# Token weights issued behind the first batch's inputs, a new landing model and two priorities, in a linear attention and mixer kernel

## The chip, the cores and the metric

The kernel runs on one core of a Trainium2 chip. The metric is the device time of one execution in microseconds (us); the lower the better. A change within 2% counts as the same. Most executions of one kernel agree within a per cent. Some fall into a slower state (over 1.5% above the fastest of the same kernel, as a rule with a lower TensorE clock).

Engine names in the profile: PE is the TensorE matmul pipeline, PEld its weight loads, DVE is VectorE, ACT is ScalarE, POOL is GpSimd, SP is SyncE, which here only issues DMAs (SPq). "L230" is a line of the kernel file that was profiled, so the same statement has different numbers in different versions.

## The reference

A gated linear attention over 4 batches, 8 heads, 768 steps and head width 48, followed by a token and channel mixer. Cut to what matters:

```python
for t in range(S):                                   # the attention, per batch and head
    state = alpha[:, :, t, :, None] * state + einsum('bhd,bhe->bhde', k[:, :, t], v[:, :, t])
    y[:, :, t] = einsum('bhd,bhde->bhe', q[:, :, t], state)
# x: y with the heads side by side, (4, 768, 384)
h  = maximum(x.T @ w_tok1, 0) @ w_tok2               # over the tokens
u  = x + h.T
out = u + maximum(u @ w_ch1, 0) @ w_ch2              # over the channels
```

Inputs and output are float32: q, k, v and alpha are 4.7 MB each.

## The kernel before

Each batch is cut into 6 chunks of 128 tokens. A chunk needs four input tiles, `at` (alpha), `kt`, `qt`, `vt`, each 128 partitions by 8 heads by 48 float32. One tile is one DMA, and in it every piece that is contiguous in memory is one row of one head, 192 bytes. The tiles land in rings of 6:

```python
inp = pool("inp", NIN)                               # NIN = 6
def load(n, name, src, after=None):
    ...
        c[name] = inp.tile([128, H, D], F32, name=name)
        nc.sync.dma_start(c[name], src[b, :, ci * C : ci * C + C, :].transpose([1, 0, 2]))
    loads[n][name] = plan.op({"SP": 550}, emit, [after], takes=[name, "loads"], lands=196608 / RATE)
```

The kernel chooses the order of instructions itself. Every piece of work is registered with `plan.op`, with its engines, modelled duration, dependencies and priority; `Plan.issue` then runs a small list scheduler while the program is built, and emits the pieces in the order that it found. Its clock is a model. An engine runs its instructions in exactly that order, so if the model believes that a tile lands earlier than it does, an engine stands in front of that tile while other work waits behind it (in run h1 below PE does so for 4.17 us). The model of a landing:

```python
if o["lands"] and eng == "POOL":                     # a weight, issued by GpSimd
    first = max(heavy, start + 2900.0)
    heavy = first + o["lands"]
    o["end"] = heavy + 900.0
    ...
elif o["lands"]:                                     # an input tile or a store, issued by SP
    wire = max(wire, start + 1650.0) + o["lands"]
    o["end"] = wire + 900.0
```

The small constants and the weights:

```python
u128 = consts.tile([128, 128], BF16, name="u128")
make_upper_triangular(nc, u128, val=1.0, diag=True)
id128 = consts.tile([128, 128], BF16, name="id128")
...
RATE = 205.0                                         # GB/s of the input tiles, in the model
...
for n in range(NT):
    ...
    pkk, vb, acqm = chunk(n)
    if n == NCH - 2:
        weight("wt1", wt1, src1, acqm, 2.6)          # first token weight, during chunk 4 of batch 0
    if n == NCH - 1:
        weight("wt2", wt2, src2, pkk, 2.3)
        weight_ch1(0, vb); weight_ch1(1, vb); weight_ch1(2, vb)
    if n == NCH:
        weight_ch2(0, vb)                            # halves of the second channel weight
    if n == NCH + 1:
        weight_ch2(1, vb)
    if NCH - 1 <= n < NT - 1:                        # batch 1's inputs wait for wt2's landing
        load_ak(n + 1, hold_back(wload["wt2"], wload["wc12"]) if n == NCH - 1 else None)
        load_qv(n + 1)
```

Of the kernel before, what the change touches and what calls it, by code (L numbers as in the profile page):

```python
# [14 lines left out]
class Plan:  # L15
# [9 lines left out]

    def __init__(self, rings, cold, window, slack):
        self.rings = rings
        self.cold = cold
        self.window = window
        self.slack = slack  # L30
        self.ops = []
        self.taken = {r: [] for r in rings}
        self.asked = {r: [] for r in rings}
        self.mixed = ("pmix", "ptp", "pcum")

    def op(self, engines, emit, deps=(), prio=0, takes=None, frees=(), lands=0.0):
        o = {"eng": engines, "emit": emit, "deps": [d for d in deps if d is not None],
             "prio": (prio, len(self.ops)), "takes": [takes] if isinstance(takes, str) else list(takes or ()), "lands": lands, "users": [],
             "end": None}
        for t in frees:  # L40
            t, only = t if isinstance(t, tuple) else (t, None)
            t["users"].append((o, only))
        for ring in o["takes"]:
            self.asked[ring].append(o)
        self.ops.append(o)
        return o

    def issue(self):
# [3 lines left out]
        while todo:  # L52
            ready = []
            for o in todo:
                if any(d["end"] is None for d in o["deps"]):
                    continue
                at = max((d["end"] for d in o["deps"]), default=0.0)
                if "PE" in o["eng"] and at > self.cold:
                    at = max(d["end"] + (0.0 if "PE" in d["eng"] else self.slack)
                             for d in o["deps"])  # L60
# [24 lines left out]
            if o["lands"] and eng == "POOL":  # L85
                first = max(heavy, start + 2900.0)
                heavy = first + o["lands"]
                o["end"] = heavy + 900.0
                wire += o["lands"]
                for p in self.ops:  # L90
                    if p["lands"] and p is not o and (p["end"] or 0.0) > first + 900.0 and "SP" in p["eng"]:
                        p["end"] += o["lands"]
            elif o["lands"]:
                wire = max(wire, start + 1650.0) + o["lands"]
                o["end"] = wire + 900.0
            else:
                o["end"] = done + self.LAG.get(eng, 0)
# [6 lines left out]
def kernel(  # L104
# [27 lines left out]
    def pool(name, bufs=1, space=None):  # L132
# [4 lines left out]
    NIN, NLA, NPK, NSS = 6, 4, 4, 3  # L137
    NAUX, NGT, NRT, NMIX = 4, 3, 24, 3
    consts = pool("consts")
    wpool = pool("wpool")  # L140
# [15 lines left out]
    ps_mix_p = pool("ps_mix", NMIX, PS)  # L156

    plan = Plan({"loads": NT * 4, "weights": 8, "at": NIN, "kt": NIN, "qt": NIN, "vt": NIN, "la": NLA, "a": NAUX,
                 "ia": NAUX, "pkq": NPK, "pkk": NPK, "vb": NAUX, "acqm": NAUX, "tp": NGT,
                 "gtm": NGT, "ss": NSS, "x": 18, "ht": 4, "u": 12, "ut": 2, "rt": NRT,  # L160
                 "o": 6, "pcum": 1, "ptp": 1, "pgt": 1, "py": 1, "pmix": NMIX}, 36000.0, {"PE": 0.0}, 600.0)

# [3 lines left out]
    u128 = consts.tile([128, 128], BF16, name="u128")  # L166
    make_upper_triangular(nc, u128, val=1.0, diag=True)
    id128 = consts.tile([128, 128], BF16, name="id128")
    make_identity(nc, id128)
# [25 lines left out]

    def weight(name, dst, src, after, us):
        def emit(e):
            gps.dma_start(dst, src)
        wload[name] = plan.op({"POOL": 1000}, emit, [after], -1, takes="weights", lands=us * 1000)
# [7 lines left out]
    def weight_ch1(g, after):  # L207
        cs = slice(g * W1C, g * W1C + W1C)
        weight(f"wc1{g}", wc1[:, :, cs], src3[:, :, cs], after, 2.2)

    def weight_ch2(g, after):
        cs = slice(g * W2C, g * W2C + W2C)
        weight(f"wc2{g}", wc2[:, cs, :], src4[:, cs, :], after, 3.6)


    RATE = 205.0
    xs = {}
# [30 lines left out]
    def chunk(n):  # L248
# [9 lines left out]
        def e_cum(e):  # L258
# [4 lines left out]
            for j in range(4):  # L263
                pe.matmul(ps[:, HD + j : HD + j + 1], lhsT=la[:, 2 * j : 2 * j + 2, :],  # L264
                          rhs=ones_col, start=True, stop=True, skip_group_check=True)
        cum = plan.op({"PE": 260}, e_cum, [ln], P, takes="pcum", frees=[ln])

        def e_ia(e):
            c["ia"] = aux.tile([128, H, D], F32, name="ia_sb")
            act.activation(c["ia"].rearrange("p h d -> p (h d)"), c["cum"][:, 0:HD], AF.Exp, scale=-1.0)  # L270
        ia = plan.op({"ACT": 375}, e_ia, [cum], P, takes="ia", frees=[cum])

        def e_a(e):
            c["a"] = aux.tile([128, HD + 4], F32, name="a_sb")
            act.activation(c["a"], c["cum"][:, 0 : HD + 4], AF.Exp)  # L275
        a = plan.op({"ACT": 375}, e_a, [cum], P, takes="a", frees=[cum])

        def e_pkk(e):
            gps.tensor_tensor(pkk_t[n % NPK][:, :, 0:D], c["kt"], c["ia"], ALU.mult)  # L279
        pkk = plan.op({"POOL": 960}, e_pkk, [l_kt, ia], P, takes="pkk", frees=[l_kt, ia])  # L280

# [50 lines left out]

        s_prev = ss_t[(n - 1) % NSS]
        s_dep = state.get(n - 1)
        if ci < NCH - 1:
# [13 lines left out]
            def e_ss(e):  # L349
                m = c["acqm"].rearrange("p j h -> p (j h)")  # L350
                dve.tensor_tensor(
                    ss_t[n % NSS], c["s"][:, 0:HD].rearrange("p (h d) -> p h d", h=H),
                    bass.AP(tensor=m.tensor, offset=m.offset,
                            ap=[list(m.ap[0]), list(m.ap[1]), [0, D]]), ALU.mult)
# [4 lines left out]
        def e_y(e):  # L359
            ps = c["y"] = ps_y_p.tile([128, H, D], F32, name="ps_y")  # L360
            for h in range(H):
# [14 lines left out]
        xop[n] = plan.op({"ACT": 375}, e_x, [y], P, takes="x", frees=[y])  # L376
        return pkk, vb, acqm

# [9 lines left out]
    def mixer(b):  # L388
# [51 lines left out]
        for g in range(NS // 2):  # L440
            hold = {}

            def e_utp(e, g=g, hold=hold):
                hold["ps"] = ps_mix_p.tile([128, 6, 128], BF16, name="ps_mm")
                for j in range(NM):
                    for i in range(2):
                        pe.transpose(hold["ps"][:, 2 * j + i, :],  # L447
                                     u[2 * g + i][:, j * 128 : (j + 1) * 128], id128)
            tj = plan.op({"PE": 330}, e_utp, us[2 * g : 2 * g + 2], TOK,
                         takes="pmix" if g else ["pmix", "ut"])  # L450

            def e_ut(e, g=g, hold=hold):
                if g == 0:
# [3 lines left out]
                    hold["ps"].rearrange("p (j i) t -> p j (i t)", i=2))  # L457
            uts.append(plan.op({"DVE": 470, "ACT": 700}, e_ut, [tj], TOK,
                               frees=[(tj, "pmix")]))
# [52 lines left out]
    for n in range(NT):  # L512
        if n + 1 < NCH:
            load_ak(n + 1)
        if n < NCH:
            load_qv(n)
        pkk, vb, acqm = chunk(n)
        if n == NCH - 2:
            weight("wt1", wt1, src1, acqm, 2.6)
        if n == NCH - 1:  # L520
            weight("wt2", wt2, src2, pkk, 2.3)
            weight_ch1(0, vb)
            weight_ch1(1, vb)
            weight_ch1(2, vb)
        if n == NCH:
            weight_ch2(0, vb)
        if n == NCH + 1:
            weight_ch2(1, vb)
        if NCH - 1 <= n < NT - 1:
            load_ak(n + 1, hold_back(wload["wt2"], wload["wc12"]) if n == NCH - 1 else None)  # L530
            load_qv(n + 1)
        if n % NCH == NCH - 1 and n >= NCH:
            mixer(n // NCH - 1)
# [33 lines left out]
```

## Time and profile before

| | before |
|---|---|
| median of the first 3 runs | 193.34 us (192.79 to 193.99) |
| span of the profiled run | 189.9 us |
| PE busy | 168.6 us, 89% |
| first token matmul / first channel matmul starts | 31.54 / 41.09 us |
| last input tile off the wire | 119.21 us |

The last line comes from the trace's records of single DMA packets: the packets of 192 bytes on the input queue, in order, are cut into groups of 1,024, one for each tile; "off the wire" is the end of the last packet of a group. Numbers for single tiles are made the same way.

The view by windows, the kernel before. Columns: window, its length, busy us (and instructions) of PE, PEld, DVE, ACT and POOL, granted PE clock, DMA share, GB/s.

```profile
0.00:31.00 31.00, 16.52 (x198) 11.77 (x199) 17.69 (x39) 11.30 (x23) 15.37 (x33) 0.87 0.99 179
40.00:50.00 10.00, 9.65 (x94) 5.99 (x93) 5.31 (x9) 8.12 (x18) 5.73 (x9) 1.00 1.03 193
50.00:60.00 10.00, 10.00 (x107) 6.29 (x105) 3.88 (x6) 8.27 (x19) 4.40 (x7) 1.00 1.21 205
60.00:80.00 20.00, 20.00 (x238) 13.28 (x237) 13.38 (x19) 8.53 (x19) 12.27 (x21) 1.00 1.02 202
80.00:100.00 20.00, 17.62 (x248) 12.30 (x246) 13.80 (x21) 14.86 (x33) 12.34 (x19) 1.00 1.02 228
100.00:120.00 20.00, 19.70 (x236) 13.42 (x234) 14.97 (x24) 15.12 (x33) 11.08 (x19) 1.00 0.89 176
```

PE's idle time is the length less the first number: 0.35, 0, 0, 2.38 and 0.30 us after 40 us. From 120 to 180 us it is zero.

The chain of waits in the start-up, the kernel before (start, length, what):

```profile
18.03 2.79 SPq L230
21.68 6.26 DMA qt<-in_q_dram
28.51 0.55 DVE ss_134 L351
29.06 1.14 DVE gtm L330
30.25 0.50 PE ps_y L362 x8
```

The last q tile of batch 0 took 6.26 us from its issue, and everything up to PE's first product of chunk 4 at 30.25 us hangs on it. The first token weight is issued by GpSimd at 21.36 us and shares the wire with it.

### The profile page before, as it was taken

The page shows a single profiled execution, that of the slowest core. Times are in us where ns is not written, and L with a number is a line of the kernel's source. Part 1 is how long each engine was busy: PE and PEld are TensorE (multiplying, and loading weights), DVE is VectorE, ACT ScalarE, POOL GpSimd, SP SyncE. Part 2 cuts the span into 40 slices and gives each one's busy share as a digit, 9 for nine tenths or more (in the row PEclk, how much of TensorE's full clock was granted, in tenths as well). Part 3 has the DMA queues.
Part 4 walks back from the last instruction along what each step waited for, and adds up shares of the span by engine and source line. Part 5 has one row for each costly group of instructions (what it writes and reads, how often), then busy time and mean ns, then how long its engine had stood idle before and what let it go on. Part 6 is the DMA issues. An engine that isn't in the chain of part 4 may idle for free.

```text
span 189.9 us, 4180 instructions
## 1 busy us (share of the span) xinstructions
PE 168.6 (89%) x1616; PEld 107.5 (57%) x1616; DVE 90.9 (48%) x152; ACT 93.7 (49%) x200; POOL 64.2 (34%) x108
## 2 busy tenths in 40 slices
PE   1377467989999999999979999999999999999992
PEld 0255344456666666657736676655665666566651
DVE  2378547172725676669734896323717102220222
ACT  3534411339885333677777588400664990059000
POOL 3643546006925555795535655500000000000000
PEclk9999955699999999999999999999999999999999
DMA  6999799999999999999999997022200001220122
GB/s 124 226 204 216 143 175 146 198 182 224 191 217 197 195 221 195 200 237 210 243 228 208 190 198 159 2 83 86 83 0 3 0 0 61 104 87 0 59 107 85
DMA packets 107139, 27.00 MB, mean 142 GB/s; under 512 B 100336, under 2 KB 107120, under 8 KB 107120
## 3 DMA queue, kind: packets, MB, share of 16 engines
q1 hardware_dynamic: 103296, 23.60, 58.1%
q0 software_dynamic: 3824, 3.15, 11.1%
q8 instruction: 12, 0.20, 0.4%
q14 instruction: 7, 0.06, 0.1%
HBM read 25.17 MB, written 4.72 MB: 157 GB/s over the span
## 4 chain that ended last, share of the span: by engine, by line
PE 70%; SPq 11%; DMA 8%; issue 3%; POOL 3%; DVE 2%; ACT 2%; POOLq 0%; DVEq 0%; ACTq 0%
PE ps_mm L492 25%; PE ps_mm L474 21%; SPq L230 11%; PE ps_mm L402 5%; PE ps_mm L426 4%; DMA qt<-in_q_dram 3%; PE gt_ps L324 3%; DMA vt<-in_v_dram 2%; DMA at<-in_alpha_dram 2%; PE ps_y L362 2%; PE ps_tp L307 2%; PE ps_mm L447 2%; PE ps_tp L312 2%; PE ps_y L367 1%; POOL pkk_131 L279 1%
## 5 line engine op out<-in xcount | busy, mean ns | idle before, releaser
L384 ACT ACTIVATE rt<-ps_mm 128x384 bf16<-128x384 f32 x90 | 43.2, 491 | 30.2 <-PE ps_mm L474 29.6
L474 PE MATMUL ps_mm<-ut,wc_156 128*128 128x384 bf16 x288 | 54.4, 326 | 0.3 <-DVE ut L455 0.3
L492 PE MATMUL ps_mm<-wc_157,rt 128*128 128x384 bf16 x288 | 49.7, 326 | 0.0
L492 PEld LDWEIGHTS <-rt 128*128 128x128 bf16 x288 | 27.3, 98 | 17.3 <-issue 0.2
L330 DVE TENSOR_TENSOR gtm<-gt_ps,u_107 128x1024 bf16<-128x1024 f32 x24 | 29.3, 1221 | 10.8 <-PE gt_ps L324 10.8
L474 PEld LDWEIGHTS <-wc_156 128*128 128x128 bf16 x288 | 25.9, 97 | 14.8 <-issue 0.8
L504 DVE TENSOR_TENSOR o_sb<-ps_mm,u_sb 128x384 f32<-128x384 f32 x24 | 13.4, 556 | 42.2 <-PE ps_mm L492 41.3
L317 DVE COPY tp<-ps_tp 128x1024 bf16<-128x1024 bf16 x21 | 14.4, 688 | 14.1 <-PE ps_tp L312 13.1
L291 POOL CAST vb<-vt 128x384 bf16<-128x384 f32 x24 | 12.1, 504 | 25.3 <-DMA vt<-in_v_dram 19.4
L375 ACT ACTIVATE x_sb<-ps_y 128x384 bf16<-128x384 f32 x24 | 11.8, 490 | 14.0 <-PE ps_y L367 13.8
L270 ACT ACTIVATE ia_sb<-ps_cum 128x384 f32<-128x384 f32 x24 | 11.8, 491 | 11.7 <-PE ps_cum L264 11.7
L433 DVE TENSOR_TENSOR u_sb<-ps_mm,x_sb 128x384 bf16<-128x384 f32 x24 | 11.8, 550 | 5.2 <-PE ps_mm L426 5.2
L402 PE MATMUL ps_mm<-x_sb,wt_154 128*128 128x384 bf16 x48 | 12.3, 375 | 0.0
L275 ACT ACTIVATE a_sb<-ps_cum 128x388 f32<-128x388 f32 x24 | 11.9, 495 | 0.0
L426 PE MATMUL ps_mm<-ht,wt_155 128*128 128x384 bf16 x48 | 10.6, 328 | 0.6 <-DVE u_sb L433 0.3
L279 POOL TENSOR_TENSOR pkk_131<-kt,ia_sb 128x384 bf16<-128x384 f32 x6 | 6.3, 1048 | 14.2 <-ACT ia_sb L270 14.2
L324 PE MATMUL gt_ps<-tp 48*128 48x128 bf16 x192 | 10.4, 233 | 0.6 <-DVE tp L317 0.4
L362 PE MATMUL ps_y<-vb,gtm 128*128 128x48 bf16 x192 | 9.3, 189 | 1.4 <-DVE gtm L330 1.4
L362 PEld LDWEIGHTS <-gtm 128*128 128x128 bf16 x192 | 8.2, 100 | 3.4 <-DVE gtm L330 2.0
L324 PEld LDWEIGHTS <-tp 48*128 48x128 bf16 x192 | 6.0, 99 | 6.2 <-issue 3.7
L279 POOL TENSOR_TENSOR pkk_130<-kt,ia_sb 128x384 bf16<-128x384 f32 x6 | 6.0, 997 | 8.8 <-ACT ia_sb L270 8.8
L279 POOL TENSOR_TENSOR pkk_129<-kt,ia_sb 128x384 bf16<-128x384 f32 x6 | 6.0, 1002 | 5.5 <-ACT ia_sb L270 5.5
(105 smaller groups left out, 195.5 us busy)
## 6 DMA issues: line engine op xcount, KB each, us to landing
at<-in_alpha_dram SPq DMA_DIRECT2D x24, 192.0 KB, 3.7
kt<-in_k_dram SPq DMA_DIRECT2D x24, 192.0 KB, 3.9
qt<-in_q_dram SPq DMA_DIRECT2D x24, 192.0 KB, 3.8
vt<-in_v_dram SPq DMA_DIRECT2D x24, 192.0 KB, 3.8
out_dram<-o_sb SPq DMA_DIRECT2D x24, 192.0 KB, 1.9
wc_156<-in_moe_w_ch_dram POOLq DMA_DIRECT2D x3, 384.0 KB, 5.9
wc_157<-in_moe_w_ch_dram POOLq DMA_DIRECT2D x2, 576.0 KB, 7.8
wt_154<-in_moe_w_tok_dram POOLq DMA_DIRECT2D x1, 384.0 KB, 6.6
```

The lines of the kernel that those rows point to most:

```text
L230: nc.sync.dma_start(c[name], src[b, :, ci * C : ci * C + C, :].transpose([1, 0, 2]))
L279: gps.tensor_tensor(pkk_t[n % NPK][:, :, 0:D], c["kt"], c["ia"], ALU.mult)
L317: (dve.tensor_copy if e == "DVE" else act.copy)(c["tp"], c["ptp"])
L324: pe.matmul(gt[:, 4 * (h % 2) + j, :], lhsT=c["tp"][base : base + D, 4 + j, :], rhs=c["tp"][base : base + D, j, :], start=True, stop=True)
L330: dve.tensor_tensor(c["gtm"], c["gt"], mask_b, ALU.mult)
L362: pe.matmul(ps[:, h, :], lhsT=c["gtm"][:, 4 * (h % 2) + h // 2, :], rhs=c["vb"][:, h, :], start=(h == 0), stop=(ci == 0 and h == H - 1), s ...
L384: act.activation(dst, ps, AF.Relu)
L402: pe.matmul(hold["ps"], lhsT=wt1[:, kc, m * 128 : (m + 1) * 128], rhs=xs[b * NCH + kc], start=(kc == 0), stop=(kc == NS - 1), skip_group_c ...
L426: pe.matmul(hold["ps"], lhsT=wt2[:, kc, i * 128 : (i + 1) * 128], rhs=ht[kc], start=(kc == 0), stop=(kc == NDT - 1))
L474: pe.matmul(hold["ps"], lhsT=wc1[:, kc, mc * 128 : (mc + 1) * 128], rhs=ut_t[0][:, kc, cs], start=(kc == 0), stop=(kc == NM - 1))
L492: pe.matmul(hold["ps"], lhsT=rt[mc][:, i * 128 : (i + 1) * 128], rhs=wc2[:, mc, :], start=(mc == 0), stop=(mc == NDC - 1), skip_group_chec ...
L504: dve.tensor_tensor(hold["o"], hold["ps"], u[i], ALU.add)
```

## The change

The intent: keep the first token weight off the wire until batch 0's inputs are through, tell the scheduler when tiles really land, and let PE transpose u as soon as it can. The diff, cut to its core:

```diff
+    psy = ps_y_p.tile([128, 512], F32, name="ps_y")       # one fixed tile for y in place of a ring of 1
+    held = consts.tile([128, 1], F32, name="held")        # right behind u128, in front of id128
     id128 = consts.tile([128, 128], BF16, name="id128")
...
-    def weight(name, dst, src, after, us):
+    def weight(name, dst, src, after, us, behind=None):
         def emit(e):
+            if behind is not None:
+                gps.tensor_copy(held, behind["ia"][:, 0, 0:1])
             gps.dma_start(dst, src)
...
         if n == NCH - 2:
-            weight("wt1", wt1, src1, acqm, 2.6)
+            loads[n]["qt"]["lull"] = 1300.0
+            early = vb
         if n == NCH - 1:
-            weight("wt2", wt2, src2, pkk, 2.3)
+            weight("wt1", wt1, src1, ia, 3.4, tiles[n])
+            ia["users"].append((wload["wt1"], None))
+            weight("wt2", wt2, src2, early, 2.9)
# landing model: inputs (and, not shown, weights: 2900 -> 2400 ns, larger times for each weight)
-    RATE = 205.0
+    RATE = 214.0
-                wire = max(wire, start + 1650.0) + o["lands"]
-                o["end"] = wire + 900.0
+                wire = max(wire, start + 1950.0) + o["lands"] + o["lull"]
+                o["end"] = wire + 700.0
# priorities (smaller is earlier): cumulative sums, their exponentials, decayed key
-        cum = plan.op({"PE": 260}, e_cum, [ln], P, ...)
+        cum = plan.op({"PE": 260}, e_cum, [ln], P - 0.3, ...)       # also ia, a, pkk
# u transposes and their copies
-            tj = plan.op({"PE": 330}, e_utp, us[2 * g : 2 * g + 2], TOK, ...)
+            tj = plan.op({"PE": 330}, e_utp, us[2 * g : 2 * g + 2], TOK - 0.3, ...)
# also: the ring index of the state tiles is n - b in place of n; from 36.5 us on (36.0 before)
# the scheduler adds its slack in front of PE
```

More of the change, by code (lines that the diff above doesn't have):

```diff
@@ L24, with __init__ @@
     LAG = {"PE": 220, "ACT": 180, "DVE": 150, "POOL": 110}
-    def __init__(self, rings, cold, window, slack):
+    def __init__(self, rings, cold, window, slack, warm):
+        self.warm = warm
         self.rings = rings
@@ L37, in op @@
         o = {"eng": engines, "emit": emit, "deps": [d for d in deps if d is not None],
-             "prio": (prio, len(self.ops)), "takes": [takes] if isinstance(takes, str) else list(takes or ()), "lands": lands, "users": [],
+             "prio": (prio, len(self.ops)), "takes": [takes] if isinstance(takes, str) else list(takes or ()), "lands": lands, "lull": 0.0, "users": [],
              "end": None}
@@ L57, in issue @@
                 at = max((d["end"] for d in o["deps"]), default=0.0)
-                if "PE" in o["eng"] and at > self.cold:
+                if "PE" in o["eng"] and at > self.warm:
                     at = max(d["end"] + (0.0 if "PE" in d["eng"] else self.slack)
@@ L85, in issue @@
             if o["lands"] and eng == "POOL":
-                first = max(heavy, start + 2900.0)
+                first = max(heavy, start + 2400.0)
                 heavy = first + o["lands"]
@@ L90, in issue @@
                 for p in self.ops:
-                    if p["lands"] and p is not o and (p["end"] or 0.0) > first + 900.0 and "SP" in p["eng"]:
-                        p["end"] += o["lands"]
+                    over = (p["end"] or 0.0) - 700.0 - first
+                    if p["lands"] and p is not o and over > 0.0 and "SP" in p["eng"]:
+                        p["end"] += o["lands"] * min(1.0, over / p["lands"])
             elif o["lands"]:
-                wire = max(wire, start + 1650.0) + o["lands"]
-                o["end"] = wire + 900.0
+                wire = max(wire, start + 1950.0) + o["lands"] + o["lull"]
+                o["end"] = wire + 700.0
             else:
@@ L138 @@
     NAUX, NGT, NRT, NMIX = 4, 3, 24, 3
+    COLD, WARM = 36500.0, 36500.0
     consts = pool("consts")
@@ L160 @@
                  "gtm": NGT, "ss": NSS, "x": 18, "ht": 4, "u": 12, "ut": 2, "rt": NRT,
-                 "o": 6, "pcum": 1, "ptp": 1, "pgt": 1, "py": 1, "pmix": NMIX}, 36000.0, {"PE": 0.0}, 600.0)
+                 "o": 6, "pcum": 1, "ptp": 1, "pgt": 1, "py": 1, "pmix": NMIX}, COLD, {"PE": 0.0}, 600.0,
+                WARM)
     act.preload_act_table_set("natural_log_exp_and_others")
@@ L208, in weight_ch1 @@
         cs = slice(g * W1C, g * W1C + W1C)
-        weight(f"wc1{g}", wc1[:, :, cs], src3[:, :, cs], after, 2.2)
+        weight(f"wc1{g}", wc1[:, :, cs], src3[:, :, cs], after, 2.8)
     def weight_ch2(g, after):
         cs = slice(g * W2C, g * W2C + W2C)
-        weight(f"wc2{g}", wc2[:, cs, :], src4[:, cs, :], after, 3.6)
-    RATE = 205.0
+        weight(f"wc2{g}", wc2[:, cs, :], src4[:, cs, :], after, 4.7)
+    RATE = 214.0
     xs = {}
@@ L265, in e_cum @@
                           rhs=ones_col, start=True, stop=True, skip_group_check=True)
-        cum = plan.op({"PE": 260}, e_cum, [ln], P, takes="pcum", frees=[ln])
+        cum = plan.op({"PE": 260}, e_cum, [ln], P - 0.3, takes="pcum", frees=[ln])
         def e_ia(e):
@@ L270, in e_ia @@
             act.activation(c["ia"].rearrange("p h d -> p (h d)"), c["cum"][:, 0:HD], AF.Exp, scale=-1.0)
-        ia = plan.op({"ACT": 375}, e_ia, [cum], P, takes="ia", frees=[cum])
+        ia = plan.op({"ACT": 375}, e_ia, [cum], P - 0.3, takes="ia", frees=[cum])
         def e_a(e):
@@ L275, in e_a @@
             act.activation(c["a"], c["cum"][:, 0 : HD + 4], AF.Exp)
-        a = plan.op({"ACT": 375}, e_a, [cum], P, takes="a", frees=[cum])
+        a = plan.op({"ACT": 375}, e_a, [cum], P - 0.3, takes="a", frees=[cum])
         def e_pkk(e):
             gps.tensor_tensor(pkk_t[n % NPK][:, :, 0:D], c["kt"], c["ia"], ALU.mult)
-        pkk = plan.op({"POOL": 960}, e_pkk, [l_kt, ia], P, takes="pkk", frees=[l_kt, ia])
+        pkk = plan.op({"POOL": 960}, e_pkk, [l_kt, ia], P - 0.3, takes="pkk", frees=[l_kt, ia])
         def e_pkq(e):
@@ L331, in chunk @@
         gtm = plan.op({"DVE": 1140}, e_gtm, [gt], P, takes="gtm", frees=[gt])
-        s_prev = ss_t[(n - 1) % NSS]
+        s_prev = ss_t[(n - 1 - b) % NSS]
         s_dep = state.get(n - 1)
@@ L351, in e_ss @@
                 dve.tensor_tensor(
-                    ss_t[n % NSS], c["s"][:, 0:HD].rearrange("p (h d) -> p h d", h=H),
+                    ss_t[(n - b) % NSS], c["s"][:, 0:HD].rearrange("p (h d) -> p h d", h=H),
                     bass.AP(tensor=m.tensor, offset=m.offset,
@@ L359, in e_y @@
         def e_y(e):
-            ps = c["y"] = ps_y_p.tile([128, H, D], F32, name="ps_y")
+            ps = c["y"] = psy[:, 0:HD].rearrange("p (h d) -> p h d", h=H)
             for h in range(H):
@@ L376, in chunk @@
         xop[n] = plan.op({"ACT": 375}, e_x, [y], P, takes="x", frees=[y])
-        return pkk, vb, acqm
+        return pkk, vb, acqm, ia
     xop = {}
@@ L448, in e_utp @@
                                      u[2 * g + i][:, j * 128 : (j + 1) * 128], id128)
-            tj = plan.op({"PE": 330}, e_utp, us[2 * g : 2 * g + 2], TOK,
+            tj = plan.op({"PE": 330}, e_utp, us[2 * g : 2 * g + 2], TOK - 0.3,
                          takes="pmix" if g else ["pmix", "ut"])
@@ L457, in e_ut @@
                     hold["ps"].rearrange("p (j i) t -> p j (i t)", i=2))
-            uts.append(plan.op({"DVE": 470, "ACT": 700}, e_ut, [tj], TOK,
+            uts.append(plan.op({"DVE": 470, "ACT": 700}, e_ut, [tj], TOK - 0.3,
                                frees=[(tj, "pmix")]))
@@ L516 @@
             load_qv(n)
-        pkk, vb, acqm = chunk(n)
+        pkk, vb, acqm, ia = chunk(n)
         if n == NCH - 2:
-            weight("wt1", wt1, src1, acqm, 2.6)
+            loads[n]["qt"]["lull"] = 1300.0
+            early = vb
         if n == NCH - 1:
-            weight("wt2", wt2, src2, pkk, 2.3)
+            weight("wt1", wt1, src1, ia, 3.4, tiles[n])
+            ia["users"].append((wload["wt1"], None))
+            weight("wt2", wt2, src2, early, 2.9)
             weight_ch1(0, vb)
```

## The prediction

> **What bounds the kernel now.** The engine table gives TensorE (PE) 168.6 us busy of 189.9. By windows, PE is busy 16.5 us in 0-31 and then almost without a gap: 9.65 of 10 in 40-50, 40 of 40 in 120-160. Its one later hole is 80-100 (17.6 of 20). So: a start-up of some 31 us fed by batch 0's inputs, a PE-bound body, a short drain. Time won before 31 us shifts the body, if no later hole takes it back.
>
> In the start-up, the chain of waits goes through the input issues to the last q tile (issued 21.68, 6.26 us to landing), then VectorE's state product and mask multiply, then PE's y product at 30.25. The DMA records show why: the first token weight is issued by GpSimd at 21.36, its packets start near 23.8, and the last q and v tiles, whose like took about 1 us each on the wire before, stretch to 3.1 and 1.5 us. The Trainium skill, "DMA: Bandwidth & Descriptors", section "Issuing engines are not separate DMA queues", says that such DMAs run on the same 16 engines and interleave; the trace agrees. Before that the engines were nearly idle for a microsecond (share 0.18 in 20-21), while an input issue took 2.79 us. The change only models that pause.
>
> **What the change does.**
> 1. wt1 waits for ia of the last chunk (ends about 23.4), so it is issued near 23.7, its packets start near 26.1 (2.4 us, as before), and it lands near 29.5-30 instead of 27.97. The last q lands near 25.4 instead of 27.94.
> 2. VectorE's wait for q (2.46 us) mostly goes. gt of chunk 4 ends at 27.0, so its mask multiply can run at 27.0-28.2 instead of 29.0-30.2, and y of chunk 4 starts near 28.3: about 2 us earlier. But token matmuls then wait for wt1: they start near 29.8 instead of 31.54. New wait on wt1: 0.2-0.8 us.
> 3. They run at half clock (windows: 0.5 from 22.9 to 36.6; 525 ns against 326). 1.7 us of earlier slow work is worth about 0.9 us of fast work. The Trainium skill, "TensorE: Matmul & The Clock Gate", Part 1, gives a free-running window of 3.4 us; the stretch of 13.65 us is four of them. A clock rise one window earlier would add up to 1.7 us, in some runs only: about 0.3 on average.
> 4. u transposes ahead of later token matmuls remove three PE waits of batch 0 (0.16, 0.23, 0.28 us): about 0.5 us. Later batches already fill them.
> 5. Added: one tiny GpSimd copy (0.2 us, off the chain).
> 6. The new landing model reorders everything after. Its 214 GB/s is more hopeful than the roughly 200-228 of all traffic, stores included, in 60-100, so PE can again stand before late tiles: -1 to +1 us.
>
> Sum: 0.9 + 0.3 + 0.5 = 1.7 us, plus about 0.9 for fewer misplaced waits in 80-100 (2.4 us idle now).
>
> **Predicted: 190.7 us, 8 in 10 between 187.8 and 193.2.** Faster by over 2%: 0.28; within 2%: 0.69; slower: 0.03.
>
> **Right or wrong by:** last q landing near 25.4; first token matmul near 29.8, held by wt1; first channel matmul near 39 instead of 41.09; time at half clock; PE idle in 80-100.
>
> **What would make it wrong:** wt1 landing past 31; batch 1's inputs so late that PE starves at 40-60; the clock rising a window earlier in most runs (faster), or later; holes in 75-100 that take the lead back.

## More of the kernel before

From the page of the profile, the kernel before: busy time of PE, then the span in 40 slices (busy tenths of PE, tenths of the granted PE clock, tenths of the mean busy share of the 16 DMA engines).

```profile
span 189.9 us, 4180 instructions
PE 168.6 (89%) x1616; PEld 107.5 (57%) x1616; DVE 90.9 (48%) x152; ACT 93.7 (49%) x200; POOL 64.2 (34%) x108
PE   1377467989999999999979999999999999999992
PEclk9999955699999999999999999999999999999999
DMA  6999799999999999999999997022200001220122
```

PE is the engine to fill: after a start-up of six slices it is nearly always busy. But the DMA engines are nearly always busy too, until slice 24, which is 119 us. There are two limits side by side.

## The result, and the profile after

The changed kernel took 202.08 us in the median of 4 runs (201.87 to 202.95), against 193.06 us for the kernel before (192.62 to 193.99): slower by 4.7%, ratio 1.0469 with a 95% interval of 1.0418 to 1.052. A ratio in this document is the mean time of one kernel's fast runs over that of the other's of the same rounds on the same chip, so it is not quite the ratio of the medians quoted. The result is correct.

The same lines of the page, the kernel after:

```profile
span 200.0 us, 4183 instructions
PE 172.5 (86%) x1616; PEld 109.4 (55%) x1616; DVE 93.6 (47%) x156; ACT 90.7 (45%) x196; POOL 65.7 (33%) x109
PE   1376789999988998685987979999999999999993
PEclk9999999999999999999999999999999999999999
DMA  7999999999999999999999999003300000420032
```

Windows of the kernel after, columns as above:

```profile
0.00:31.00 31.00, 18.25 (x186) 12.55 (x186) 17.76 (x38) 11.50 (x23) 15.88 (x33) 1.00 1.19 166
40.00:50.00 10.00, 9.72 (x84) 6.34 (x83) 3.05 (x7) 8.13 (x19) 3.85 (x6) 1.00 1.12 186
50.00:60.00 10.00, 9.29 (x97) 5.80 (x94) 4.82 (x7) 6.96 (x16) 5.68 (x9) 1.00 1.25 197
60.00:80.00 20.00, 18.53 (x226) 12.28 (x225) 12.91 (x19) 8.68 (x19) 10.65 (x17) 1.00 1.11 180
80.00:100.00 20.00, 15.41 (x215) 10.92 (x216) 14.20 (x22) 9.71 (x22) 11.75 (x18) 1.00 1.11 215
100.00:120.00 20.00, 16.73 (x191) 10.57 (x190) 12.01 (x19) 11.06 (x27) 9.96 (x18) 1.00 1.16 189
```

PE now idles 1.47, 4.59 and 3.27 us in the last three windows, 9.3 us in place of 2.7. The DMA engines are busier (1.19 for 0.99 in the start-up) and move less (166 GB/s for 179). That pair of numbers is the clue: more time for each byte.

One column needs care. The clock is printed as 1.00 wherever the trace has no clock record, and the kernel after has none before 37.09 us. Its matmuls are slow up to there: the 12 token matmuls of 128x384 between 32 and 37 us take 514 ns in the mean, and 326 ns later. The kernel before has its first record at 16.08 us, full clock to 22.91 and half clock to 36.56 us. So the clock rises for good at nearly the same time in both (36.56 and 37.09 us), neither falls again before 190 us, and the clock does not explain the loss.

The chain of waits of the kernel after, between 76 and 111 us, runs almost entirely through alpha tiles:

```profile
76.85 8.92 DMA at<-in_alpha_dram x2
86.76 9.29 DMA at<-in_alpha_dram x2
96.55 3.94 DMA at<-in_alpha_dram
103.11 7.46 DMA at<-in_alpha_dram x2
110.65 0.53 ACT la_123 L264
```

The packet records say when it starts. Wire time of the first 20 input tiles, us from the start of one tile to the next, with nothing but input tiles on the wire:

```
tile         0    1    2    3    4    5    6    7    8    9   10   11   12   13   14   15   16   17   18   19
before     1.03 0.98 0.90 0.98 0.86 0.85 0.81 0.87 0.82 0.91 0.96 0.95 1.16 0.82 0.87 0.97 0.85 0.95 0.96 2.28
after      1.02 0.89 0.94 1.05 1.03 1.05 1.06 1.05 1.06 1.05 1.06 1.05 1.05 1.06 1.07 1.05 1.04 1.06 1.09 1.74
```

Before any part of the new order can matter, from the fourth tile on, the kernel after is tied to 1.05 us a tile (187 GB/s), where the kernel before takes 0.81 to 1.16, mostly 0.9. The median duration of one packet is 15 ns before and 22 to 24 ns after. A new order of instructions can hardly do that at 5 us (run 2 below tests it). The last q tile of batch 0 is off the wire at 26.33 us in place of 26.89, so the start-up's gain is nearly all eaten there; the first channel matmul starts at 41.99, later than the 41.09 of before. And the last input tile of all is off the wire at 125.54 us, 6.3 us later than before; from there to the end it takes 74.5 us, 3.8 us more than the 70.7 of before. 6.3 and 3.8 make the 10.1 us by which the spans differ, to rounding. So there are two losses to explain: a slower input stream, and more PE work left over when it ends.

**Where the slower stream may come from.** The change adds one thing in front of every other tile on chip: `held`, a tile of 4 bytes per partition. In the compiled programs it takes 32 bytes, and all later tiles move by 32. The `at`, `kt`, `qt` and `vt` tiles start at multiples of 64 before (56,512 for the first `at`), and 32 past one after (56,544). The rows of 192 bytes within a tile keep that remainder, because 192 is a multiple of 64. That was a suspicion, not yet a cause.

### The profile page after: what moved, and what is told of

The parts are those of the page before. It is cut to its first block, busy times and chain, and to the rows that moved or that the text cites. A ratio compares the mean times of both kernels' runs of the same rounds, so it can differ in the third digit from the quotient of the medians.

```text
span 200.0 us, 4183 instructions
## 1 busy us (share of the span) xinstructions
PE 172.5 (86%) x1616; PEld 109.4 (55%) x1616; DVE 93.6 (47%) x156; ACT 90.7 (45%) x196; POOL 65.7 (33%) x109
## 4 chain that ended last, share of the span: by engine, by line
PE 50%; DMA 27%; SPq 10%; ACT 3%; POOL 3%; DVE 3%; issue 2%; POOLq 0%; ACTq 0%; DVEq 0%
PE ps_mm L501 20%; DMA at<-in_alpha_dram 20%; PE ps_mm L483 17%; SPq L239 10%; DMA wc_159<-in_moe_w_ch_dram 5%; PE ps_mm L411 3%; PE ps_mm L435 3%; DMA vt<-in_v_dram 2%; PE gt_ps L333 2%; PE ps_tp L321 1%; PE ps_mm L456 1%; PE ps_y L371 1%; DVE gtm L339 1%; PE ps_cum L270 1%; ACT rt L393 1%
## 5 line engine op out<-in xcount | busy, mean ns | idle before, releaser
L393 ACT ACTIVATE rt<-ps_mm 128x384 bf16<-128x384 f32 x89 | 42.7, 493 | 19.3 <-PE ps_mm L483 18.9
L326 DVE COPY tp<-ps_tp 128x1024 bf16<-128x1024 bf16 x22 | 15.1, 686 | 17.0 <-PE ps_tp L321 17.0
```

Source lines behind the costliest of these rows:

```text
L326: (dve.tensor_copy if e == "DVE" else act.copy)(c["tp"], c["ptp"])
L393: act.activation(dst, ps, AF.Relu)
```

## The experiments

Theories: *placement* (the 32 bytes slow the writes of the input DMAs), *order* (the new landing model and priorities put PE in front of tiles that are still on the way), and *late weights* (the weights, or batch 1's inputs behind them, now come too late). Eighteen kernels ran. "Realigned change" is the changed kernel with `held` widened to 64 bytes.

The runs of the whole kernel in one table (the four of loads alone are in section 4). PE idle times are from the windows of each profiled run; "channel" is the start of the first channel matmul.

| run | ratio to before | 95% interval | channel, us | PE idle 40-50 | 50-60 | 60-120 |
|---|---|---|---|---|---|---|
| before | 1 | | 41.09 | 0.35 | 0.00 | 2.68 |
| after | 1.0469 | 1.0418-1.052 | 41.99 | 0.28 | 0.71 | 9.33 |
| e1_before_plus_held | 1.0278 | 1.0191-1.0365 | (profile slow) | | | |
| e3_only_inputs_shifted | 1.0336 | 1.0283-1.0389 | 41.93 | 0.36 | 1.47 | 7.53 |
| e2_after_held64 | 1.0159 | 1.0099-1.0219 | 39.85 | 0.19 | 1.08 | 5.86 |
| f1_old_landing | 1.0009 | 0.9949-1.007 | 39.92 | 0.08 | 2.31 | 4.18 |
| f2_old_prio | 1.0102 | 1.0018-1.0185 | (profile slow) | | | |
| f3_old_utp | 1.0104 | 1.0061-1.0148 | 38.01 | 0.19 | 0.82 | 4.67 |
| f5_oldland_oldprio | 1.0015 | 0.9969-1.006 | 38.54 | 0.07 | 2.60 | 2.28 |
| h1_wc2_one_earlier | 1.0034 | 0.9947-1.0122 | 37.33 | 2.15 | 4.17 | 2.04 |
| h2_wc2_both_earlier | 1.0047 | 0.9947-1.0147 | 37.88 | 0.65 | 1.92 | 3.67 |
| k1_half_wc2 | 0.9837 | 0.9752-0.9921 | 37.66 | 0.07 | 0.40 | 5.58 |
| p1_late_weights_alone | 0.9975 | 0.991-1.0041 | 38.22 | 0.07 | 2.52 | 3.06 |
| f6_190_oldprio | 0.9907 | 0.9832-0.9982 | 37.84 | 0.07 | 3.27 | 2.15 |
| q1_before_rate190 | 0.9914 | 0.9865-0.9963 | (profile slow) | | | |
| q2_late_weights_rate190 | 0.993 | 0.9885-0.9975 | 39.18 | 0.07 | 2.88 | 2.25 |

### 1. The tile alone, on the kernel before

```diff
     make_upper_triangular(nc, u128, val=1.0, diag=True)
+    held = consts.tile([128, 1], F32, name="held")
+    dve.memset(held, 0.0)
```

> The kernel before with nothing but the change's 4-byte tile added among the constants (it takes 32 bytes, so every later on-chip tile starts 32 past a multiple of 64 instead of on one); same instruction order. Placement theory: most of the loss comes from this alone: 199 to 203 us, and a backlogged input tile takes about 1.05 us on the wire as in the changed kernel, instead of 0.8 to 0.95. Order theory (the new schedule and the later weights make PE wait): 193 us, as before.

Measured: 198.94, 199.39 and 201.55 us in its fast runs, median of before 194.33 us, ratio 1.0278. The packet records of its slow profile show the expected 1.04 to 1.07 us a tile on the wire. The unused tile alone costs nearly 3%. The placement theory holds; the order theory had expected 193 us.

### 2. The change with the tile widened to 64 bytes

```diff
-    held = consts.tile([128, 1], F32, name="held")
+    held = consts.tile([128, 16], F32, name="held")
-                gps.tensor_copy(held, behind["ia"][:, 0, 0:1])
+                gps.tensor_copy(held[:, 0:1], behind["ia"][:, 0, 0:1])
```

> The changed kernel with the tile widened from 4 to 64 bytes, so that all input tiles start on multiples of 64 again; instruction order identical to the changed kernel on all engines. Placement theory: the loss goes, 189 to 193 us, and the last q tile lands near 25.4 as predicted. Order theory: 202 us, as after.

Measured: 197.56 us (196.74 to 197.84), ratio 1.0159. The instruction order is the same as in the changed kernel on all engines, yet the ratio falls from 1.0469 by 0.031. Tiles on the wire are back at 0.81 to 1.1 us with packets of 15 ns, the last q tile of batch 0 is off the wire at 24.54 us and the first channel matmul starts at 39.85. But the expected 189 to 193 us did not come: half of my placement theory, that it is the whole loss, is wrong. 1.6% is left. The window of the start-up of this run, columns as above (after: DMA share 1.19, 166 GB/s):

```profile
0.00:31.00 31.00, 18.34 (x208) 13.17 (x209) 18.19 (x40) 11.80 (x24) 16.56 (x34) 0.90 0.96 177
```

### 3. Only the input tiles shifted, on the kernel before

```diff
+    padlo = pool("padlo")
     inp = pool("inp", NIN)
+    padhi = pool("padhi")
+    lo = padlo.tile([128, 8], F32, name="lo")     # 32 bytes in front of the input tiles
+    hi = padhi.tile([128, 8], F32, name="hi")     # 32 bytes behind: later tiles move by 64 in all
```

> The kernel before with 32 bytes of padding in front of the input tiles and 32 behind them: only the landing tiles of the input DMAs are off the multiples of 64, weights, stores and all other operands are as before. If the slow writes of the input DMAs are the cause: the same as the first of these runs within 1%, 199 to 203 us. If operands of the compute engines, the weights or the output stores carry part of it: clearly between 193 and that.

Measured: 201.09 us (200.74 to 201.46), ratio 1.0336; the intervals of this and of run 1 overlap. Shifting only the places where the input DMAs land does all of it. Weights, stores and the tiles that engines write are not needed for the loss. Nor did the engines get slower at reading the shifted tiles: GpSimd's product of k and the decay took 998 ns (997 to 1048 before). The start-up of this run (before: 0.99, 179 GB/s):

```profile
0.00:31.00 31.00, 18.17 (x186) 12.81 (x186) 15.56 (x40) 11.52 (x23) 13.26 (x30) 1.00 1.17 168
```

### 4. The loads by themselves

Two kernels with a wrong result: nothing but the 96 input loads into 24 tiles and 24 stores, with all tiles on multiples of 64 or 32 bytes past one.

```diff
-    lead = pl.tile([128, 32], F32, name="lead")   # 128 bytes: tiles on multiples of 64
+    lead = pl.tile([128, 24], F32, name="lead")   # 96 bytes: tiles 32 past a multiple of 64
     tiles = [inp.tile([128, H, D], F32, name=f"t{i}") for i in range(24)]
     ... 96 times: nc.sync.dma_start(tiles[i % 24], ...)
```

> Wrong result on purpose: only the 96 input loads into 24 tiles that start on multiples of 64, then 24 stores. Placement theory: 0.83 to 0.92 us for each load, the packets 15 ns each, 96 loads in 80 to 88 us.

> Wrong result on purpose: the same loads with all 24 tiles 32 bytes past a multiple of 64. Placement theory: 1.05 us for each load from about the fourth on, packets 22 to 24 ns, 96 loads in 99 to 102 us; the two differ by 12 to 18 us. If the placement only matters beside the compute engines, the two are the same.

A window of the aligned loads, then one of the shifted loads (busy DVE and POOL, PE clock, DMA share, GB/s):

```profile
10.00:90.00 80.00, 0.00 (x0) 0.00 (x0) 1.00 1.08 214
```

```profile
10.00:80.00 70.00, 0.00 (x0) 0.00 (x0) 1.00 1.45 187
```

214 against 187 GB/s, at a DMA share of 1.08 against 1.45. The tile-by-tile records of the shifted loads are as expected, 1.05 us from the fourth tile to the 77th with hardly an exception. The aligned loads are a little slower than expected: 0.80 to 1.15 us a tile, and 89.0 us for all 96 in place of 80 to 88. The last load ends at 90.83 and 103.33 us, the whole kernels took 105.63 and 118.48 us: 12.9 us, or 12%, for 32 bytes. No compute engine takes part. (One run each.)

**Why 32 bytes may matter.** In both kernels the rows of a tile start at four different places modulo 256, since 192 is not a multiple of 256: 0, 64, 128 and 192 in the fast one, 32, 96, 160 and 224 in the slow one. The Trainium skill, "DMA: Bandwidth & Descriptors", section "How a descriptor splits into AXI transactions", states transactions of at most 256 bytes that start at 256-byte boundaries. So a row that crosses a boundary takes two. Of the four starts, two cross in the fast kernel (128 and 192) and three in the slow one (96, 160 and 224): six transactions for four rows against seven. That is an estimate from the page of 7/6 = 1.17. The expectations below count the page's beats of 32 bytes instead, from the boundary below a row's start, 40/36 = 1.11, also an estimate. The two rates measured here differ by 1.14 and don't choose between the two counts. A rival account was pieces of 64 bytes: three whole pieces for an aligned row, two whole and two half ones for a shifted row. Two more kernels tell them apart, with each row landing at a pitch of 256 bytes, so that no row crosses a boundary, and all rows starting at 0 or at 32 modulo 256.

```diff
-    tiles = [inp.tile([128, H, D], F32, name=f"t{i}") for i in range(24)]
+    tiles = [inp.tile([128, H, 64], F32, name=f"t{i}") for i in range(24)]
-            nc.sync.dma_start(tiles[i % 24], src[...])
+            nc.sync.dma_start(tiles[i % 24][:, :, 0:D], src[...])
```

> Wrong result on purpose: the 96 loads alone again, but each row of 192 bytes lands at a pitch of 256 bytes, all rows starting on multiples of 256. Two accounts of the placement loss. If writes pay for beats from the 256-byte boundary below a row's start (36 beats for four rows in the aligned loads, 40 in the shifted ones, an estimate of 11% more), this needs only 24 and is clearly faster than 214 GB/s if the writes set the pace. If only whole or half pieces of 64 bytes count, it is as the aligned loads: 210 to 216 GB/s.

> Wrong result on purpose: as the run before, all rows starting 32 past a multiple of 256. Boundary account: 28 beats for four rows, fewer than the 36 of the aligned loads, so at least 214 GB/s. Piece account (three whole pieces of 64 bytes become two whole and two half): 187 GB/s, as the shifted loads.

Windows of m2, then of m3:

```profile
10.00:80.00 70.00, 0.00 (x0) 0.00 (x0) 1.00 1.09 215
```

```profile
10.00:80.00 70.00, 0.00 (x0) 0.00 (x0) 1.00 1.07 211
```

Rows that start 32 bytes past a multiple of 64 are fast, 211 GB/s, if they land at a pitch of 256 bytes and cross no boundary. The account by pieces of 64 bytes, as it was put, falls. The account by 256-byte boundaries also missed once: m2, with four transactions for four rows in place of six, was to be clearly faster if the writes set the pace, and is no faster than m0 (215 against 214 GB/s). It can stand only with a bound: on this account the writes don't set the pace at six or below; something else does, at some 214 GB/s. (Reading may: the rows in memory are 192 bytes at a pitch of 192, too, which by the same count are six for four rows. No run shows it.)

So the reason is not shown. Half of m0's rows cross a boundary, and yet 98% of its packets in the backlog take 15 ns, as in m2, where none crosses. And a rival is untested: in m1 every row shares a piece of 64 bytes with the next row, and in m3, with gaps between the rows, none does. Rows at a pitch of 256 that start at 128 modulo 256 would tell the two apart: each crosses a boundary, and no two share a piece. What the runs do show is that 32 bytes of shift, with rows at a pitch of 192 bytes, cost the loads 214 against 187 GB/s.

The stores of these two kernels are cut into rows of 192 bytes and slower, so their whole times, 118.63 and 119.9 us, say nothing about the loads.

### 5. What is left: landing model, priorities, transposes

All on the realigned change.

```diff
# f1_old_landing (f5 has both of these, too)
-    RATE = 214.0
+    RATE = 205.0
-                wire = max(wire, start + 1950.0) + o["lands"] + o["lull"]
-                o["end"] = wire + 700.0
+                wire = max(wire, start + 1650.0) + o["lands"] + o["lull"]
+                o["end"] = wire + 900.0
# f2_old_prio (f5, too): cum, ia, a, pkk at P in place of P - 0.3
# f3_old_utp: u transposes and their copies at TOK in place of TOK - 0.3
```

> The realigned changed kernel (which took 1.016 times the time of before) with the input tiles' landing model of before: 205 instead of 214 GB/s, 1650 and 900 ns instead of 1950 and 700; everything else of the change kept. Hopeful-landing theory (PE is placed in front of alpha tiles that are still on the way): 1.000 to 1.005 of before, and PE's wait of 10.1 us on the cumulative sums shrinks by half. Priority theory (the 0.3 of priority given to the cumulative sums does it) or late-weights theory: stays at 1.012 to 1.02.

> The realigned changed kernel with the priority of the cumulative sums, their two exponentials and the decayed key put back (no 0.3 ahead); the hopeful landing model kept. Priority theory: 0.995 to 1.005 of before, PE's wait on the cumulative sums about 4 us in place of 10.1. Hopeful-landing or late-weights theory: stays at 1.012 to 1.02.

> The realigned changed kernel with the u transposes back behind the token matmuls. My prediction gave the transposes about 0.5 us: if so this is slower than the realigned change, 1.018 to 1.02 of before. If the transposes are a cause of the loss: 1.010 or less. If they do nothing: 1.016.

> The realigned changed kernel with both the landing model of the inputs and the priorities of before: what is left of the change is the late weights and their landing times, the modelled pause and the u transposes. If the whole remaining loss comes from landing model and priority: 0.990 to 0.998 of before (the start-up's gain of about 1.2 us is left). If the late weights themselves cost (channel weights or batch 1's inputs late): 1.01 or more.

Measured: f1 194.62 us (193.34 to 195.47), 1.0009. f2 197.19 (194.53 to 199.16, the last slow), 1.0102. f3 196.42 (195.76 to 196.84), 1.0104. f5 194.55 (194.0 to 195.38), 1.0015, all against 194.44.

The landing model of the inputs alone brings back the 1.5%. Of the three it is the only one whose interval lies wholly below that of run 2 (which ran on another chip, against the kernel before there); the intervals of f2 and f3 also touch that of f1. f5 was expected at 0.990 to 0.998 and came out at 1.0015. The priorities and the transposes are not settled by one run each: either, put back, gave some 0.5%, but their intervals overlap that of run 2, and with the old landing model the priorities change nothing (1.0009 and 1.0015). My finer expectation, that PE's wait on the cumulative sums halves, failed: it went from 10.1 to 8.8 us. Two lines of the waits, first of the realigned change, then of f1 (who waited for whom: total us, times, longest):

```profile
ACT la L264 <- DMA at<-in_alpha_dram: 21.6, 14, 3.1
PE ps_cum L270 <- ACT la L264: 10.1, 7, 4.2
```

```profile
ACT la L264 <- DMA at<-in_alpha_dram: 15.2, 13, 2.8
PE ps_cum L270 <- ACT la L264: 8.8, 6, 4.1
```

Some 4 us of the second line is a wait at the very start in every version (4.1 us is the longest one). What fell is PE's idle time in 60 to 120, from 5.86 to 4.18 us, spread over cumulative sums, key transposes and score products that stood in front of late tiles. But in 50 to 60 it rose from 1.08 to 2.31 us, so that from 40 to 120 only 0.6 us is gained. That the landing model costs the time is measured; that it costs it through PE in front of late tiles is shown only in part.

f5 also shows that the start-up does gain: its first channel matmul starts at 38.54 us in place of 41.09, a lead of 2.5 us. At the end nothing is left of it. The loss of the lead shows in 50 to 60 us, where before there was no idle time (windows and wait of f5):

```profile
50.00:60.00 10.00, 7.40 (x74) 4.42 (x72) 2.08 (x3) 5.09 (x12) 3.00 (x5) 1.00 1.14 185
60.00:80.00 20.00, 19.65 (x231) 12.78 (x229) 13.48 (x20) 8.28 (x19) 11.83 (x18) 0.91 0.96 189
```

```profile
PE ps_mm L501 <- DMA wc<-in_moe_w_ch_dram: 2.6, 2, 2.3
```

PE now reaches the second channel weight before its second half has landed (58.5 us, both before and now).

The clock took a share that the table leaves out. The 0.91 in 60 to 80 is a stretch at half clock from 60.23 to 63.65 us, right behind f5's hole; matmuls of 128x384 take up to 528 ns in it, and 326 outside. An estimate from these: 3.4 us at half clock cost PE up to 1.7 us. Run 2 has such a stretch too (89.52 to 92.93 us) and f3 one of twice the length (76.64 to 83.46), but the kernel before and f1 have none behind the start-up. So a part of what run 2 lost against f1, and of what f5 lost of its lead, may be the clock. There is one profile of each, and no run separates it. Nor is there a rule in it: the kernel after, with 4.59 us of idle time in 80 to 100, keeps its clock.

### 6. That weight earlier

On f5: the two halves issued one chunk earlier each (h1), or both straight behind the first channel weight (h2).

```diff
             weight_ch1(2, vb)
+            weight_ch2(0, vb)
         if n == NCH:
-            weight_ch2(0, vb)
-        if n == NCH + 1:
             weight_ch2(1, vb)
```

> The realigned change with the landing model and priorities of before (1.0015 of before), and the two halves of the second channel weight issued one chunk earlier each. In the run without this, the channel matmuls start 2.5 us earlier than before (38.5 against 41.1) but PE then stands 2.6 us on the second channel weight in 50 to 60. Given-back theory (the start-up's gain turns into a wait for that weight): the wait falls below 1 us and the time to 0.987 to 0.995 of before. If the gain is lost elsewhere (inputs of batch 1 late, luck of the order): stays at 0.998 to 1.005.

> As the run before, with both halves of the second channel weight issued straight behind the first channel weight, before any input of batch 1. The wait for it goes to zero; but batch 1's inputs start about 6 us later. If the body has room for that: 0.985 to 0.995 of before. If the body hangs on the input stream: 1.005 or more, with new holes in 45 to 100.

Measured: 195.48 us (1.0034) and 195.53 us (1.0047) against 194.7. PE's wait for the weight is gone in both profiles, and the time did not fall. In h1 the hole merely changed its owner: PE now stands 4.17 us in one piece, until 56.80 us, in front of an alpha tile of batch 1 (windows and wait of h1):

```profile
40.00:50.00 10.00, 7.85 (x60) 4.63 (x59) 1.93 (x4) 6.96 (x17) 3.92 (x6) 1.00 0.99 180
50.00:60.00 10.00, 5.83 (x52) 3.32 (x50) 3.70 (x6) 3.65 (x8) 3.18 (x6) 0.85 1.04 182
```

```profile
PE ps_cum L270 <- ACT la L264: 11.6, 5, 4.2
```

The weight and the inputs draw on the same DMA engines, whose share is about 1 here: what one gets earlier, the other gets later.

### 7. Less to load

Wrong result, on f5: only the first half of the second channel weight is loaded and used twice. PE's work stays, 1.18 MB of reading goes.

```diff
-        if n == NCH + 1:
-            weight_ch2(1, vb)
...
-                pe.matmul(..., rhs=wc2[:, mc, :], ...)
+                pe.matmul(..., rhs=wc2[:, mc % W2C, :], ...)
```

> Wrong result on purpose: the realigned change with the landing model and priorities of before (1.0015 of before), but only the first half of the second channel weight is loaded and used twice, so 1.18 MB less is read by the DMA engines around 50 to 58 while PE's work stays the same. Supply theory (the start-up's lead is lost because the DMA engines can't deliver both that weight and batch 1's inputs any sooner): PE's idle time in 50 to 60 falls from 2.6 us to under 1 and the time to 0.975 to 0.99 of before. If the lead is lost to the order alone: 0.995 to 1.005.

Measured: 191.18 us (190.34 to 192.07) against 193.57, ratio 0.9837. PE's idle time in 50 to 60 falls from 2.60 to 0.40 us, and the last input tile is off the wire at 116.34 us in place of 119.40. Windows of this run:

```profile
50.00:60.00 10.00, 9.60 (x105) 6.18 (x104) 4.74 (x7) 6.09 (x14) 4.15 (x7) 1.00 1.06 194
60.00:80.00 20.00, 18.59 (x217) 12.31 (x216) 11.94 (x18) 10.21 (x21) 12.71 (x21) 1.00 0.99 198
```

The lead survives when the DMA engines have less to do. That is what the supply theory expects for the hole in 50 to 60 us. The size of the gain is not the lead alone: the order of instructions differs here too, since the scheduler sees the missing weight, and the half-clock stretch of f5 is missing (1.00 in 60 to 80). Nor is it shown that supply sets the pace all the way to 119 us: in f1 and in q2 below the last input tile is off the wire at 122.32 and 122.80 us, later than before, and they take 1.0009 and 0.993.

### 8. The late weights alone, and a sober rate

p1 is f5 with the u transposes put back as well. f6 is the realigned change with the old priorities and `RATE = 190.0`. q1 is the kernel before with `RATE = 190.0` and nothing else. q2 is p1's parts (late weights, old priorities, old transposes) on the landing constants of the change with `RATE = 190.0`.

> The realigned change with the landing model, the priorities and the u transposes all as before: only the late token weights with their own landing times and the modelled pause are left. If the u transposes are worth the 0.5 us that I gave them: 1.003 to 1.006 of before. If they do harm, as undoing them alone suggested (1.0104 against 1.0159): 0.995 to 0.999.

> The realigned change with the priorities of before and an input rate of 190 GB/s in the model, below what the traces show, in place of 214. Hopeful-landing theory: a sober rate does at least as well as 205, 0.99 to 1.002 of before, with little PE waiting on cumulative sums after 40 us. If only luck of the order counts: anywhere between 0.99 and 1.02.

> The kernel before with nothing but the planner's input rate lowered from 205 to 190 GB/s. If the gain of the last 190 GB/s run (0.9907 of before) came from the sober rate alone: 0.988 to 0.994. If the late token weights are needed for it: 0.996 to 1.004.

> The realigned late token weights, priorities and u transposes as before, 190 GB/s in the model: the best of the parts found, as a version to beat both kernels. If rate and late weights both count: 0.985 to 0.993 of before. If the order's luck rules: anywhere from 0.99 to 1.005.

Measured: p1 193.56 us (0.9975) and f6 192.41 us (0.9907), both against 193.57; q1 193.1 us (0.9914) and q2 192.99 us (0.993), both against 194.53. The waits of f6:

```profile
PE ps_cum L270 <- ACT la L264: 5.4, 2, 4.0
ACT la L264 <- DMA at<-in_alpha_dram: 3.7, 3, 1.6
```

With 190 GB/s in the model, ScalarE's wait for alpha is 3.7 us; with 214 it was 21.6 in run 2, and 21.9 in f2, which has f6's priorities. Lowering the rate helps the kernel before by 0.9% all by itself (q1), and the late weights add nothing to it that shows (q2, f6: the intervals overlap). The u transposes show no effect of their own: 0.9975 without and 1.0015 with them, 0.993 without and 0.9907 with them, within the intervals. f6, q1 and q2, with intervals wholly below 1, are versions that beat both kernels, by under 1%, which counts as the same here.

## Why the prediction was wrong

I predicted 190.7 us, with 0.03 for a loss of more than 2%; it was 202.08.

1. **Step 5, "Added: one tiny GpSimd copy (0.2 us, off the chain)", is where it failed.** I costed the instruction and not the tile that it writes. The copy does take 0.19 us and harms nothing. The tile takes 32 bytes in front of all others, and that slows every backlogged input tile to 1.05 us: 1.0469 with it and 1.0159 without it in the changed kernel, 1.0278 from it alone in the kernel before, 1.0336 from shifting only the input tiles. About two thirds of the loss.
2. **Step 6, the landing model, was seen with the right sign as a risk and booked the wrong way.** I wrote that 214 GB/s was hopeful, gave it -1 to +1 us, and then added 0.9 us of gain for "fewer misplaced waits in 80-100". Measured: undoing the inputs' landing model moves the ratio from 1.0159 to 1.0009, so it cost 1.5%, about 2.9 us by the medians of before (in part perhaps through the clock, section 5). PE's idle time in 80 to 100 was 2.82 us in the realigned change; it was 2.38 before.
3. **Steps 1 to 3, the start-up, were right once the tiles are realigned.** I expected the last q tile to land near 25.4 us; it is off the wire at 24.54 in run 2 and 24.10 in f5 (before, landing came 1.05 us behind the wire: 27.94 and 26.89). I expected the first channel matmul near 39; 39.85 and 38.54. The first token matmul, expected near 29.8 and held by its weight, starts at 30.70 and 29.11 in these two, and the longest wait for that weight is 0.2 us. In the changed kernel itself the slower wire ate the gain: 32.81 us for the first token matmul and 41.99 for the first channel matmul.
4. **The sum was wrong in supposing that such a lead reaches the end.** I read PE as the limit after 31 us, and named "holes in 75-100 that take the lead back" only as a danger. The lead of 2.5 us in f5 is gone by 60 us, in a hole of 2.60 us in front of the second channel weight. Moving that weight (h1, h2) did not help and taking half of it away (k1) did, which points to the DMA engines, at a share of about 1, as the limit there. The warning stood in the profile before: the DMA row is as full as PE's until slice 24.
5. **Step 4, the u transposes:** 0.5 us was expected; no effect outside the intervals was found in either direction.

I had cited the Trainium skill, "DMA: Bandwidth & Descriptors", section "Issuing engines are not separate DMA queues", for the start-up. Runs h1, h2 and k1 agree with the same statement in the body, where I had not applied it: the time did not fall when the weight was issued earlier (1.0034 and 1.0047), and fell when half of it went (0.9837).

Still open: why the shift by 32 bytes slows the writes (boundaries of 256 bytes, or rows that share a piece of 64); what holds the aligned loads at 214 GB/s; how much the half-clock stretches took; whether the priorities or the transposes cost anything with the hopeful landing model (f2, f3); and how much of any one ratio is the luck of one order, since each edit reshuffles thousands of instructions.

## What to carry to other kernels

A new tile costs more than its instruction: it moves every tile behind it, so compare the on-chip addresses of DMA targets before and after a change, and put odd little tiles last or pad them, so that the targets keep their places (here multiples of 64). Where two rows of the profile are full, ask whether time saved on one is kept: here the lead of 2.5 us was lost until the DMA engines had less to do. A scheduler's model did better here a little late than a little early: 190 GB/s gave 0.9914 and 205 GB/s 1 in the kernel before; in the realigned change 214 gave 1.0159 and 205 gave 1.0009.

## What the Trainium skill lacked or had wrong

- Speed by the start of an on-chip DMA target. "SBUF — State Buffer", section "Operand start alignment", says that it "is about legality, not speed" and that its runs "timed nothing". Here rows of 192 bytes loaded at 214 GB/s when they started on multiples of 64 and at 187 GB/s when they started 32 past one; 105.63 against 118.48 us for loads and stores alone.
- "DMA: Bandwidth & Descriptors", section "How a descriptor splits into AXI transactions", speaks of reading and gives no speed. The runs fit its count on the writing side with a bound (six transactions for four rows at 214 GB/s, seven at 187, four at 215 and 211), but don't prove it: rows that share a piece of 64 bytes are a rival that no run excludes.
- No page says that a small constant tile can slow the DMAs of a whole kernel: 4 bytes, rounded up to 32, cost 2.8% (run 1).
- "TensorE: Matmul & The Clock Gate", Part 1, warns that clock events in traces have been seen to be unreliable. No run here shows that. The kernel after's views print 1.00 before 37.09 us because its trace has no clock record there, and its matmuls fit the records: 514 ns for the token matmuls of 128x384 between 32 and 37 us, 326 ns for the same shape later.
